# Softplus from one table function, and an LN root by Newton steps, in a fused attention and two-MLP kernel

## Chip, cores and metric

One core of a Trainium2 chip runs the kernel. The metric is device microseconds, the median of three runs. The five engines each run their own queue of instructions in order: TensorE (PE, with its weight loads as PEld), VectorE (DVE), ScalarE (ACT), GpSimd (POOL) and SyncE (SP), which issues the DMAs.

## The reference

Windowed attention, then an MLP with SoLU and layer norm, then an MLP with softplus:

```python
# q, k, v: 4 batches, 8 heads, 576 positions, 64 wide
scores = where(mask, q @ k.T / 8, -1e9)       # heads 0-3: window of 32
attn = softmax(scores); x = attn @ v          # heads 4-7: every 4th of 128
x = x reshaped to 2304 tokens x 512
h = x @ w_in1                                 # 512 x 1024
solu = h * softmax(h)
ln = (solu - mean) / sqrt(var + 1e-6) * g_ln
y = ln @ w_out1                               # 1024 x 512
h = y @ w_in2                                 # 512 x 2048
g = maximum(h, 0) + log1p(exp(-abs(h)))       # softplus
out = g @ w_out2                              # 2048 x 512
```

## The kernel before, in words

All matrices are split into a high and a low fp16 half, and each product is three matmuls (high x high, high x low, low x high). Weights are read raw, converted and scaled by VectorE and ScalarE, and kept in SBUF as fp16 halves (tile W, tile E and parts of W as working room). Attention runs in 28 pairs of blocks; `pair` takes the first ten in fp32 (`pair32`, `block32`) and the others in fp16 halves (`block`). A block has scores on TensorE, a mask and maximum on VectorE (L990), four Exp on ScalarE (`expo`, L885 and L995), halves of the result, transposed matrices by a DMA on SP's queue, values on TensorE, and a normalization.

Tokens then go through `m1` (L1075), 18 tiles of 128 tokens: 24 matmuls into a two-bank PSUM tile ps_w, a maximum (L1116), an Exp with sum (L1119), products, a Square with sum for the variance (L1127), and the root of the variance: ScalarE takes Ln and Exp of a single column (L1131 and L1132), VectorE adds one Newton step (L1134 to L1137). A normalization and a transposing DMA (lnT) follow. `y_stage` (L1160) makes y for groups of 256 tokens.

`mlp2` (L1194) does the second MLP: nine groups of 256 tokens, eight steps p each, 72 steps. A step is `hidden` (24 matmuls of 256 columns into one of two PSUM banks that y, too, uses), then the softplus into g, then `outp` (12 matmuls of 512 columns into ps_w). The softplus is seven operations: Abs (L1223, ScalarE, bank to tile a, scale invC), ReLU (L1225, ScalarE or VectorE, bank to tile r, scale KR), Exp and Ln on a (L1232 and L1233), a VectorE pass that forms KR * a + r in r (L1234), the high half of r in g as a cast (L1235, ScalarE or VectorE) and the low half r - g (L1236, VectorE). There are two buffers of a, two of r, three of g. The first two groups (`early`) take their scales by weight quarter (KR0, invD), the others one scale (KR, iD).

The order of all instructions is made by a planner, `Plan`, when the program is built. Each operation has the engines it can run on with a cost, operations it comes after, and buffers it uses. Selected steps have a due time, from the table `DUE` (L303): the pairs, m1 tiles, y, the hidden steps by weight quarter, and the weight quarters. `order` (L141) hands the due times back along the dependences and then simulates: whenever an engine is idle it takes the most urgent ready operation for which buffers are free. Where TensorE has nothing to do in the first 400 us of that simulation, eight small matmuls are put in as fillers (L1337). Every engine's queue, SP's DMAs too, follows the list that comes out; after L1332 the operations are issued in that order.

Helpers record the operations, so their lines show in the profile: L464 all ScalarE ACTIVATEs, L468 and L470 VectorE tensor_scalar, L473 scalar_tensor_tensor, L476 tensor_tensor, L497 casts, L482 matmuls, L485 transposes. The table of ScalarE's functions is loaded once, at L521.

Of the kernel before, what the change touches and what calls it, by code (L numbers as in the profile page):

```python
# [10 lines left out]
FP32 = mybir.dt.float32  # L11
# [5 lines left out]
AXX = mybir.AxisListType.X  # L17
NEG = -(2.0 ** 120)
# [42 lines left out]
class Op:  # L61
    __slots__ = ("name", "opts", "fn", "after", "uses", "due", "late", "i", "wait", "succ", "mv", "cols", "on", "t0", "t1")


class Plan:
# [11 lines left out]
    SAME = {"PE": 0.0, "ACT": 0.105, "DVE": 0.08}  # L77

# [62 lines left out]
    def order(self):  # L141
# [14 lines left out]
        moved = 0.0  # L156
        self.acts, self.fast, self.known, self.dense = [0.0], [False], [0], []
# [6 lines left out]
        while events:  # L164
# [17 lines left out]
            while again:  # L182
                again = False
                for e in self.ENGINES:
# [81 lines left out]
def kernel(  # L266
# [104 lines left out]
    KR0 = mem([128, 2, NQ], FP32, "KR0")  # L371
    KR = mem([128, 2, NQ], FP32, "KR")
# [59 lines left out]
    a_pool = pool("a", 2, [128, 2, GRP], FP32, fifo=False)  # L432
    r_pool = pool("r", 2, [128, 2, GRP], FP32, fifo=False)
# [87 lines left out]
    nc.scalar.preload_act_table_set("natural_log_exp_and_others")  # L521
# [165 lines left out]
    def w2_quarter(qd, wait_i, wait_o):  # L687
# [18 lines left out]
            lambda e: stt(KR0[:, 0, c], s2o[:, 1, c], 2.0 ** 50, t[:, 1:2], ALU.mult, ALU.mult),  # L706
            lambda e: ts(KR0[:, 1, c], KR0[:, 0, c], invC[:, c]),
        )]
        if qd == NQ - 1:
# [3 lines left out]
                lambda e: ts(KR[:, 0], s2o[:, 1], 2.0 ** 50, t[:, 2:3], ALU.mult, ALU.mult),  # L713
                lambda e: tt(KR[:, 1], KR[:, 0], invC, ALU.mult),
# [153 lines left out]
    def block32(n, o, kind, b, i, half, rows, m, nk, qt, kt, v3, qk_ops, v_ops, due):  # L868
# [16 lines left out]
        def expo(e):  # L885
# [6 lines left out]
            (act_cost(nk, ptr=1, psum=1, k=4), expo),  # L892
# [79 lines left out]
    def block(n, o, kind, b, i, half, rows, m, nk, sc, qt, kt, v2, at, qk_ops, v_ops, due, x2s):  # L972
# [22 lines left out]
        def expo(e):  # L995
# [7 lines left out]
            (act_cost(nk, ptr=1, k=4), expo),  # L1003
# [71 lines left out]
    def m1(t):  # L1075
# [31 lines left out]
        if iv is None:  # L1107
# [11 lines left out]
        ex = P.op(f"m1e{t}", act_cost(F1, ptr=2, acc=1, psum=1), lambda e: act(eb.t, ph(), ACTF.Exp, scale=x(), bias=col(1), accum_out=col(2)), after=[mx], uses=[ps, st, eb])  # L1119
# [19 lines left out]
        c1 = P.op(f"m1x{t}", TINY, lambda e: ts(col(11), col(4), col(10)), after=[cf], uses=[st])  # L1139
        c2 = P.op(f"m1y{t}", TINY, lambda e: ts(col(12), col(5), col(10)), after=[cf], uses=[st])  # L1140
# [53 lines left out]
    def mlp2(j):  # L1194
# [6 lines left out]
        for p in range(NP):  # L1201
# [5 lines left out]
            ps, ab, rb, gb = Buf(ps_y), Buf(a_pool), Buf(r_pool), Buf(g_pool)  # L1207
# [162 lines left out]
```

## Time and profile before

| | us |
|---|---|
| median of three runs | 772.73 (770.56 to 773.54) |
| span of the profiled execution, first to last instruction | 767.3 |
| TensorE busy | 722.2 |
| VectorE busy | 571.1 |
| ScalarE busy | 488.7 |

The profile is of one execution; its own time is known as its span. Busy time of TensorE counts matmuls that wait in a pipeline, so a high share is not yet full speed.

### The profile page before, as it was taken

Reading aid. Unit: us, or ns where it says so; the run is one execution under the profiler, and the core shown is the slowest. Engines: PE = TensorE matmul, PEld = TensorE weight load, DVE = VectorE, ACT = ScalarE, POOL = GpSimd, SP = SyncE. Lnnn points to the kernel's source line nnn. Section 1 sums busy time; section 2 is a strip of 40 time slices with the busy share of each in tenths; the row PEclk is TensorE's granted clock in tenths of the full one; section 3 lists DMA queues with packets and bytes.
Section 4 is the critical chain, followed back from the end, with each engine's and each line's share of the span. In section 5 each row is a group of like instructions: output and inputs, shape, how many; then the busy total and the mean of one; then the engine's idle time right before and its main releaser. Section 6 shows DMA issues by size and latency. Waiting matters only on the chain.

```text
span 767.3 us, 16330 instructions
## 1 busy us (share of the span) xinstructions
PE 722.2 (94%) x6233; PEld 516.2 (67%) x6233; DVE 571.1 (74%) x1628; ACT 488.7 (64%) x1090; POOL 3.5 (0%) x22
## 2 busy tenths in 40 slices
PE   7999789999889999989989889999999999999997
PEld 6775566767766657867646567658577576767654
DVE  2899789889999997899879999984456726433334
ACT  4576865688897777898749868964437415452513
POOL 1000000000000000000000000000000000000000
PEclk9558888999999999999999999999999999999999
DMA  9986763465977345998987787630411012000001
GB/s 212 286 270 191 195 184 90 138 129 136 177 149 133 119 122 175 208 199 157 162 161 150 125 155 138 114 59 15 109 29 28 1 24 60 1 1 1 1 28 56
DMA packets 187806, 89.94 MB, mean 117 GB/s; under 512 B 158032, under 2 KB 175440, under 8 KB 187728
## 3 DMA queue, kind: packets, MB, share of 16 engines
q1 hardware_dynamic: 187728, 88.90, 51.7%
q8 instruction: 49, 0.80, 0.4%
q14 instruction: 29, 0.24, 0.1%
HBM read 54.53 MB, written 4.72 MB: 77 GB/s over the span
## 4 chain that ended last, share of the span: by engine, by line
PE 48%; DVE 28%; ACT 9%; DMA 6%; issue 5%; SPq 1%; ACTq 0%; DVEq 0%
PE bank L482 24%; PE ps_w L482 21%; DVE W L473 5%; DVE E L473 3%; DMA pT<-p 2%; PE bank L1337 2%; ACT a L464 2%; DVE s L990 2%; ACT s L464 1%; DVE st L1116 1%; DVE r L473 1%; DMA E<-in_moe_w_out_dram 1%; DVE p L476 1%; ACT E L464 1%; DVE E L470 1%
## 5 line engine op out<-in xcount | busy, mean ns | idle before, releaser
L482 PEld LDWEIGHTS <-W 128*128 128x128 f16 x2592 | 252.4, 98 | 38.9 <-issue 3.8
L482 PE MATMUL bank<-y,W 128*128 128x256 f16 x1728 | 196.6, 274 | 3.2 <-ACT a L464 2.1
L482 PE MATMUL ps_w<-W,g 128*128 128x512 f16 x864 | 195.5, 382 | 0.5 <-DVE osb L468 0.5
L482 PEld LDWEIGHTS <-g 128*128 128x128 f16 x864 | 83.8, 99 | 94.6 <-issue 2.9
L482 PE MATMUL ps_w<-W,xr 128*128 128x512 f16 x432 | 103.3, 396 | 1.2 <-DVE osb L468 0.6
L482 PE MATMUL bank<-lnT,W 128*128 128x256 f16 x864 | 97.6, 273 | 0.0
L464 ACT ACTIVATE a<-a 128x512 f32<-128x512 f32 x144 | 90.3, 627 | 2.5
L464 ACT ACTIVATE a<-bank,invC 128x512 f32<-128x512 f32 x72 | 49.1, 681 | 64.8 <-PE bank L482 61.4
L482 PEld LDWEIGHTS <-xr 128*128 128x128 f16 x432 | 43.2, 102 | 53.1 <-issue 9.1
L473 DVE SCALAR_TENSOR_TENSOR r<-a,KR,r 128x512 f32<-128x512 f32 x72 | 53.5, 744 | 18.3 <-ACT r L464 10.5
L464 ACT ACTIVATE E<-E 128x768 f32<-128x768 f32 (+3 forms) x56 | 40.8, 729 | 27.2 <-DVE E L473 16.7
L1337 PE MATMUL bank<-eye 128*128 128x60 bf16 x1056 | 42.9, 201 | 15.6 <-DVE rs L468 4.9
L470 DVE TENSOR_SCALAR r<-bank,KR 128x512 f32<-128x512 f32 x33 | 24.7, 748 | 43.2 <-ACT a L464 38.6
L464 ACT ACTIVATE s<-s 96x128 f32<-96x128 f32 (+3 forms) x144 | 43.6, 376 | 15.7 <-DVE s L470 9.5
L1337 PEld LDWEIGHTS <-eye 128*128 128x128 bf16 x1056 | 40.3, 105 | 18.3 <-issue 18.1
L476 DVE TENSOR_TENSOR g<-r,g 128x512 f16<-128x512 f32 x72 | 49.3, 685 | 2.9
L497 DVE CAST g<-r 128x512 f16<-128x512 f32 x52 | 21.9, 422 | 31.5 <-PE ps_w L482 31.0
L464 ACT ACTIVATE r<-bank,KR 128x512 f32<-128x512 f32 x39 | 26.6, 682 | 22.8 <-DVE g L476 22.8
L990 DVE CUSTOM_DVE_ANT_0 s<-bank,band,bsc 96x128 f32<-96x128 f32 (+3 forms) x144 | 38.8, 321 | 0.7 <-DVE x L476 0.2
L482 PE MATMUL bank<-kT,qT 128*96 128x128 f16 (+7 forms) x304 | 29.9, 246 | 4.5 <-DVE s L990 3.7
L464 ACT ACTIVATE e<-ps_w,st,bsc 128x1024 f32<-128x1024 f32 x16 | 19.2, 1199 | 18.8 <-DVE st L468 11.2
L464 ACT ACTIVATE y<-bank 128x512 f16<-128x512 f32 x17 | 9.9, 587 | 31.4 <-PE bank L482 31.4
(199 smaller groups left out, 949.1 us busy)
## 6 DMA issues: line engine op xcount, KB each, us to landing
E<-in_moe_w_in_dram SPq DMA_DIRECT2D x18, 512.0 KB, 4.6
E<-in_moe_w_out_dram SPq DMA_DIRECT2D x18, 512.0 KB, 4.6
out_dram<-osb SPq DMA_DIRECT2D x18, 256.0 KB, 2.0
E<-in_q_dram SPq DMA_DIRECT2D x9, 384.0 KB, 3.2
E<-in_k_dram SPq DMA_DIRECT2D x9, 384.0 KB, 3.5
E<-in_v_dram SPq DMA_DIRECT2D x9, 384.0 KB, 3.4
W<-in_moe_w_in_dram SPq DMA_DIRECT2D x6, 512.0 KB, 5.5
W<-in_moe_w_out_dram SPq DMA_DIRECT2D x6, 512.0 KB, 5.3
```

Source lines behind the costliest of these rows:

```text
L464: pin(nc.scalar.activation(out=out, in_=in_, func=func, **kw))
L470: pin(nc.vector.tensor_scalar(out=out, in0=in0, scalar1=s1, scalar2=s2, op0=op0, op1=op1))
L473: pin(nc.vector.scalar_tensor_tensor(out=out, in0=in0, scalar=s, in1=in1, op0=op0, op1=op1, **kw))
L476: pin(nc.vector.tensor_tensor(out=out, in0=a, in1=b, op=op))
L482: pin(nc.tensor.matmul(out, l, r, start=start, stop=stop))
L497: pin(nc.vector.tensor_copy(out, in_))
L990: pin(nc.vector.tensor_tensor_reduce(out=sv()[:rows, h, :nk], in0=sb.t[:rows, h, :nk], in1=band[:rows, 48 - m:48 - m + nk], scale=sc[:rows ...
L1116: ({"DVE": (1.142, 0.14)}, lambda e: pin(nc.vector.tensor_reduce(out=col(0), in_=ph(), axis=AXX, op=ALU.max, negate=True)), [mb], [ps]),
L1337: pin(nc.tensor.matmul(banks[1][:, 452:512], eye, eye[:, 0:60], start=False, stop=False, skip_group_check=True))
```

## The change

The softplus of a step becomes three operations: Softplus on ScalarE (bank to r, scale invC), the high half scaled by KR, the low half KR * r - g on VectorE. The a buffers go, the r buffers become four. Softplus is in another table than Exp, so operations can name a table; the planner keeps track of the one loaded, charges 1.4 us for a switch (SWITCH) and treats an operation of the other table as 20 us less urgent (CLING), and a load is issued at each switch. The LN root is done by VectorE alone: a first guess by an integer shift, then three Newton steps. The due times are all new.

```diff
+TABLES = {1: "exp_and_others", 2: "softplus"}
...
+    SWITCH = 1.4
+    CLING = 20.0
...
-                    for k, (_, i) in enumerate(ready[e]):
+                    best = None
+                    for key, i in ready[e]:
                         o = self.ops[i]
+                        if best is not None and key >= best[0]:
+                            break
+                        if e == "ACT" and o.tab and o.tab != tab:
+                            key += self.CLING
+                            if best is not None and key >= best[0]:
+                                continue
...
+                    if e == "ACT" and o.tab and o.tab != tab:
+                        c += self.SWITCH
+                        tab = o.tab
...
-        "pair0": -306.26, "pair1": 456.13, "pair2": 383.87, "pair3": -398.59, "pair4": 207.99, "pair5": 302.62,
+        "pair0": 1047.13, "pair1": 1033.87, "pair2": 1015.4, "pair3": 1200, "pair4": 58.3, "pair5": 619.87,
...
-    KR0 = mem([128, 2, NQ], FP32, "KR0")
-    KR = mem([128, 2, NQ], FP32, "KR")
+    KR0 = mem([128, NQ], FP32, "KR0")
+    KR = mem([128, NQ], FP32, "KR")
...
-    a_pool = pool("a", 2, [128, 2, GRP], FP32, fifo=False)
-    r_pool = pool("r", 2, [128, 2, GRP], FP32, fifo=False)
+    r_pool = pool("r", 4, [128, 2, GRP], FP32, fifo=False)
...
-    nc.scalar.preload_act_table_set("natural_log_exp_and_others")
+    nc.scalar.preload_act_table_set("exp_and_others")
...
-            lambda e: stt(KR0[:, 0, c], s2o[:, 1, c], 2.0 ** 50, t[:, 1:2], ALU.mult, ALU.mult),
-            lambda e: ts(KR0[:, 1, c], KR0[:, 0, c], invC[:, c]),
+            lambda e: stt(KR0[:, c], s2o[:, 1, c], 2.0 ** 50, t[:, 1:2], ALU.mult, ALU.mult),
...
-        v1 = P.op(f"m1w{t}", dve_cost(0), lambda e: ts(col(7), col(6), 1.0 / F1, 1e-6, ALU.mult, ALU.add), after=[va], uses=[st])
-
-        rt = P.chain(f"m1r{t}", [
-            ({"ACT": (0.094, 0.15)}, lambda e: act(col(8), col(7), ACTF.Ln)),
-            ({"ACT": (0.094, 0.15)}, lambda e: act(col(9), col(8), ACTF.Exp, scale=-0.5)),
-        ], after=[v1], uses=[st])
+        i32 = lambda i: col(i).bitcast(INT32)
         cf = P.chain(f"m1k{t}", [(TINY, f) for f in (
+            lambda e: ts(col(7), col(6), 1.0 / F1, 1e-6, ALU.mult, ALU.add),
+            lambda e: ts(i32(9), i32(7), 1, op0=ALU.logical_shift_right),
+            lambda e: ts(i32(9), i32(9), -1.0, float(0x5F3759DF - 2 ** 31), ALU.mult, ALU.add),
             lambda e: stt(col(10), col(9), col(9), col(7), ALU.mult, ALU.mult),
-            lambda e: ts(col(10), col(10), -512.0, 1536.0, ALU.mult, ALU.add),
-            lambda e: ts(col(10), col(10), col(9)),
-        )], after=[rt], uses=[st])
+            lambda e: stt(col(9), col(10), 3.0, col(9), ALU.subtract, ALU.mult),
+            lambda e: stt(col(10), col(9), col(9), col(7), ALU.mult, ALU.mult),
+            lambda e: stt(col(9), col(10), 12.0, col(9), ALU.subtract, ALU.mult),
+            lambda e: stt(col(10), col(9), col(9), col(7), ALU.mult, ALU.mult),
+            lambda e: stt(col(10), col(10), 768.0, col(9), ALU.subtract, ALU.mult),
+        )], after=[va], uses=[st])
...
-            ab_ = P.op(f"ab{j}.{p}", act_cost(512, ptr=1, psum=1), lambda e, ps=ps, ab=ab, cq=cq: act(ab.t, ps.t, ACTF.Abs, scale=invC[:, cq]), after=[hm], uses=[ps, ab])
...
-            re = P.op(f"re{j}.{p}", {**act_cost(512, ptr=1, psum=1), **dve_cost(512, x=1.5)}, relu, after=[hm], uses=[ps, rb])
-            ee = P.op(f"ee{j}.{p}", act_cost(512), lambda e, ab=ab: act(ab.t, ab.t, ACTF.Exp, scale=-1.0), after=[ab_], uses=[ab])
-            le = P.op(f"le{j}.{p}", act_cost(512), lambda e, ab=ab: act(ab.t, ab.t, ACTF.Ln, bias=1.0), after=[ee], uses=[ab])
-            fi = P.op(f"gf{j}.{p}", dve_cost(512, x=1), lambda e, ab=ab, rb=rb, cq=cq, kr=kr: stt(rb.t, ab.t, kr[:, 0, cq], rb.t, ALU.mult, ALU.add), after=[le, re], uses=[ab, rb])
-            gh = P.op(f"gh{j}.{p}", either(512), lambda e, rb=rb, gb=gb: cast(e, gb.t[:, 0], rb.t), after=[fi], uses=[rb, gb])
-            gl = P.op(f"gl{j}.{p}", dve_cost(512), lambda e, rb=rb, gb=gb: tt(gb.t[:, 1], rb.t, gb.t[:, 0], ALU.subtract), after=[gh], uses=[rb, gb])
+            sp = P.op(
+                f"sp{j}.{p}", act_cost(512, ptr=1, psum=1),
+                lambda e, ps=ps, rb=rb, cq=cq: act(rb.t, ps.t, ACTF.Softplus, scale=invC[:, cq]), after=[hm], uses=[ps, rb], tab=2,
+            )
+            gh = P.op(
+                f"gh{j}.{p}", either(512, ptr=1),
+                lambda e, rb=rb, gb=gb, cq=cq, kr=kr: scaled(e, gb.t[:, 0], rb.t, kr[:, cq]), after=[sp], uses=[rb, gb],
+            )
+            gl = P.op(
+                f"gl{j}.{p}", dve_cost(512, x=1),
+                lambda e, rb=rb, gb=gb, cq=cq, kr=kr: stt(gb.t[:, 1], rb.t, kr[:, cq], gb.t[:, 0], ALU.mult, ALU.subtract),
+                after=[gh], uses=[rb, gb],
+            )
...
+        if o.on == "ACT" and o.tab and o.tab != tab:
+            tab = o.tab
+            pin(nc.scalar.preload_act_table_set(TABLES[tab]))
         o.fn(o.on)
```

The attention's Exp and the first MLP's Exp (L892, L1003, L1119) name table 1.

## Rows read from the trace of the kernel before

**Rows 1.** Busy time by stretch: stretch, its length, busy us of each engine (instructions), clock.

```profile
0.00:100.00 100.00, 85.07 (x743) 65.72 (x744) 75.47 (x200) 65.26 (x190) 3.52 (x22) 0.73 0.81 227
100.00:200.00 100.00, 92.75 (x941) 70.87 (x940) 92.33 (x289) 71.33 (x178) 0.00 (x0) 0.93 0.58 138
200.00:505.00 305.00, 286.90 (x2716) 203.15 (x2715) 277.80 (x896) 243.92 (x542) 0.00 (x0) 0.99 0.76 150
505.00:767.30 262.30, 257.51 (x1836) 176.49 (x1836) 125.47 (x248) 108.17 (x182) 0.00 (x0) 1.00 0.12 29
```

The engines stand in the order PE, PEld, DVE, ACT, POOL; after the clock come the DMA share and GB/s.

**Rows 2.** Chain of waits, shares by line, from 200 to 505 us and from 505 us.

```profile
by line: PE ps_w L482 12.1%; PE bank L482 12.1%; issue 8.5%; DMA pT<-p 5.4%; ACT a L464 4.2%; DVE s L990 3.7%; DVE E L473 3.4%; ACT s L464 3.2%; DVE W L473 2.4%; DVE r L473 2.3%; DVE p L476 2.2%; PE bank L1337 2.1%; DVE st L1116 1.9%; DMA E
...
by line: PE bank L482 51.8%; PE ps_w L482 46.4%; DVE osb L468 0.3%; ACT osb L464 0.3%; issue 0.0%
```

**Rows 3.** Busy time by stretch of the filler matmuls' line L1337 alone: PE, PEld.

```profile
100.00:200.00 100.00, 10.90 (x281) 10.13 (x281) 0.93 0.58 138
200.00:505.00 305.00, 13.49 (x432) 12.76 (x431) 0.99 0.76 150
```

**Rows 4.** Groups of instructions the change removes or alters: busy us, mean ns, idle before.

```profile
L464 ACT ACTIVATE a<-a 128x512 f32<-128x512 f32 x144 | 90.3, 627 | 2.5
L473 DVE SCALAR_TENSOR_TENSOR r<-a,KR,r 128x512 f32<-128x512 f32 x72 | 53.5, 744 | 18.3 <-ACT r L464 10.5 <-ACT a L464 7.7
L476 DVE TENSOR_TENSOR g<-r,g 128x512 f16<-128x512 f32 x72 | 49.3, 685 | 2.9
L464 ACT ACTIVATE a<-bank,invC 128x512 f32<-128x512 f32 x72 | 49.1, 681 | 64.8 <-PE bank L482 61.4 <-DVE r L473 1.7 <-DVE r L470 1.6
L464 ACT ACTIVATE r<-bank,KR 128x512 f32<-128x512 f32 x39 | 26.6, 682 | 22.8 <-DVE g L476 22.8
L470 DVE TENSOR_SCALAR r<-bank,KR 128x512 f32<-128x512 f32 x33 | 24.7, 748 | 43.2 <-ACT a L464 38.6 <-PE bank L482 3.4
L464 ACT ACTIVATE st<-st 128x1 f32<-128x1 f32 x36 | 7.0, 195 | 1.1 <-DVE st L470 0.7
```

**Rows 5.** Groups that resemble what is added, and the casts of before.

```profile
L497 DVE CAST g<-r 128x512 f16<-128x512 f32 x52 | 21.9, 422 | 31.5 <-PE ps_w L482 31.0
L464 ACT ACTIVATE g<-r 128x512 f16<-128x512 f32 x20 | 12.4, 619 | 2.6 <-DVE r L473 2.4
L473 DVE SCALAR_TENSOR_TENSOR W<-E,s2o,W 128x512 f16<-128x512 f32 x16 | 11.2, 743 | 0.0
L464 ACT ACTIVATE W<-E,s2o 128x512 f16<-128x512 f32 x11 | 7.2, 708 | 0.0
L473 DVE SCALAR_TENSOR_TENSOR st<-st 128x1 f32<-128x1 f32 x36 | 6.4, 178 | 1.6 <-ACT st L464 1.4
L468 DVE TENSOR_SCALAR W<-E,s2o 128x512 f16<-128x512 f32 x5 | 2.2, 480 | 0.0
```

**Rows 6.** Busy time by stretch of tile KR's instructions, then of tile a's: DVE, ACT.

```profile
200.00:505.00 305.00, 36.55 (x55) 11.57 (x17) 0.99 0.76 150
...
200.00:505.00 305.00, 23.66 (x33) 62.75 (x99) 0.99 0.76 150
```

**Rows 7.** Tile hl from 200 to 505 us: ns min/median/max, first and last start.

```profile
L464 ACT ACTIVATE hl<-e,st x9: 1226/1237/1254, 206.5 to 483.1; 128x1024 f16<-128x1024 f32 x9
```

**Rows 8.** Timeline of ScalarE, its first instruction: start us, duration us.

```profile
0.80 1.28 ACT L521 ACT_TABLE_LOAD   x1 [0.80 <-PEq L1354]
```

**Rows 9.** Timeline of ScalarE: Abs and attention's Exp in turn, first and last.

```profile
205.96 0.69 ACT L464 ACTIVATE a<-bank,invC 128x512 f32<-128x512 f32 x1 [0.43 <-PE bank L482]
...
208.86 1.23 ACT L464 ACTIVATE s<-s 80x112 f32<-80x112 f32 x4
...
499.60 0.67 ACT L464 ACTIVATE a<-bank,invC 128x512 f32<-128x512 f32 x1
```

**Rows 10.** Chain of waits in order of time: start us, us, the two longest waits on weight loads.

```profile
68.91 3.59 DMA E<-in_moe_w_out_dram
...
139.34 4.88 DMA E<-in_moe_w_out_dram
```

More of the change, by code (lines that the diff above doesn't have):

```diff
@@ L61 @@
 class Op:
-    __slots__ = ("name", "opts", "fn", "after", "uses", "due", "late", "i", "wait", "succ", "mv", "cols", "on", "t0", "t1")
+    __slots__ = ("name", "opts", "fn", "after", "uses", "due", "late", "i", "wait", "succ", "mv", "cols", "tab", "on", "t0", "t1")
 class Plan:
@@ L81, in __init__, with op @@
         self.due = due
-    def op(self, name, opts, fn, after=(), uses=(), due=None, mv=0, cols=0.0):
+    def op(self, name, opts, fn, after=(), uses=(), due=None, mv=0, cols=0.0, tab=0):
         o = Op()
-        o.name, o.opts, o.fn, o.due, o.mv, o.cols = name, opts, fn, due, mv, cols
+        o.name, o.opts, o.fn, o.due, o.mv, o.cols, o.tab = name, opts, fn, due, mv, cols, tab
         o.after = [a for a in dict.fromkeys(after) if a is not None]
@@ L102, in chain @@
             w = [*(after if o is None else [o]), *(more[0] if more else [])]
-            o = self.op(f"{name}{'abcdefghijklmnop'[i]}", opts, fn, w, [*uses, *(more[1] if len(more) > 1 else [])])
+            o = self.op(f"{name}{'abcdefghijklmnop'[i]}", opts, fn, w, [*uses, *(more[1] if len(more) > 1 else [])], tab=more[2] if len(more) > 2 else 0)
         return o
@@ L156, in order @@
         moved = 0.0
+        tab = 1
         self.acts, self.fast, self.known, self.dense = [0.0], [False], [0], []
@@ L196, in order @@
                                 continue
-                        got = []
+                        got, slots = [], []
                         for b in o.uses:
@@ L205, in order @@
                                 got.append(b)
+                                slots.append(s)
                         else:
-                            break
+                            best = (key, o, list(zip(got, slots)))
                         for b in reversed(got):
@@ L210, in order @@
                             b.pool.next -= 1
-                    else:
+                        if best is not None and e != "ACT":
+                            break
+                    if best is None:
                         continue
+                    _, o, got = best
+                    i, c = o.i, o.opts[e][0]
+                    for b, s in got:
+                        b.slot, s[4][0] = s, True
+                        b.pool.next += 1
                     for f in o.opts:
@@ L712, in w2_quarter @@
                 lambda e: recip(t[:, 2:3], iD),
[L713 to L714 removed]
+                lambda e: ts(KR, s2o[:, 1], 2.0 ** 50, t[:, 2:3], ALU.mult, ALU.mult),
             )]
@@ L891, in block32 @@
             (TINY, lambda e: ts(nm()[:rows], mx()[:rows], -scale)),
-            (act_cost(nk, ptr=1, psum=1, k=4), expo),
+            (act_cost(nk, ptr=1, psum=1, k=4), expo, [], [], 1),
         ], after=[qk_mm], uses=[sb, s2])
@@ L1002, in block @@
             (TINY, lambda e: ts(nm()[:rows], mx()[:rows], -1.0, shift, ALU.mult, ALU.add)),
-            (act_cost(nk, ptr=1, k=4), expo),
+            (act_cost(nk, ptr=1, k=4), expo, [], [], 1),
         ], after=[mk], uses=[s2])
@@ L1118, in m1 @@
         ], after=[iv_ok[b0], iv_ok[b1]], uses=[st])
-        ex = P.op(f"m1e{t}", act_cost(F1, ptr=2, acc=1, psum=1), lambda e: act(eb.t, ph(), ACTF.Exp, scale=x(), bias=col(1), accum_out=col(2)), after=[mx], uses=[ps, st, eb])
+        ex = P.op(f"m1e{t}", act_cost(F1, ptr=2, acc=1, psum=1), lambda e: act(eb.t, ph(), ACTF.Exp, scale=x(), bias=col(1), accum_out=col(2)), after=[mx], uses=[ps, st, eb], tab=1)
         rc = P.chain(f"m1c{t}", [
@@ L1206, in mlp2 @@
                 po = Buf(ps_w)
-            ps, ab, rb, gb = Buf(ps_y), Buf(a_pool), Buf(r_pool), Buf(g_pool)
+            ps, rb, gb = Buf(ps_y), Buf(r_pool), Buf(g_pool)
             cq = slice(qd, qd + 1)
@@ L1222, in mlp2 @@
             hm = P.op(f"h{j}.{p}", pe_cost(2.62), hidden, cols=6.1, after=[*y_ops[j], *need], uses=[ps, yb], due=(f"h{j}.{qd}", d))
-            ab_ = P.op(f"ab{j}.{p}", act_cost(512, ptr=1, psum=1), lambda e, ps=ps, ab=ab, cq=cq: act(ab.t, ps.t, ACTF.Abs, scale=invC[:, cq]), after=[hm], uses=[ps, ab])
-            def relu(e, ps=ps, rb=rb, cq=cq, kr=kr):
-                if e == "ACT":
-                    act(rb.t, ps.t, ACTF.Relu, scale=kr[:, 1, cq])
-                else:
-                    ts(rb.t, ps.t, kr[:, 1, cq], 0.0, ALU.mult, ALU.max)
-            re = P.op(f"re{j}.{p}", {**act_cost(512, ptr=1, psum=1), **dve_cost(512, x=1.5)}, relu, after=[hm], uses=[ps, rb])
-            ee = P.op(f"ee{j}.{p}", act_cost(512), lambda e, ab=ab: act(ab.t, ab.t, ACTF.Exp, scale=-1.0), after=[ab_], uses=[ab])
-            le = P.op(f"le{j}.{p}", act_cost(512), lambda e, ab=ab: act(ab.t, ab.t, ACTF.Ln, bias=1.0), after=[ee], uses=[ab])
-            fi = P.op(f"gf{j}.{p}", dve_cost(512, x=1), lambda e, ab=ab, rb=rb, cq=cq, kr=kr: stt(rb.t, ab.t, kr[:, 0, cq], rb.t, ALU.mult, ALU.add), after=[le, re], uses=[ab, rb])
-            gh = P.op(f"gh{j}.{p}", either(512), lambda e, rb=rb, gb=gb: cast(e, gb.t[:, 0], rb.t), after=[fi], uses=[rb, gb])
-            gl = P.op(f"gl{j}.{p}", dve_cost(512), lambda e, rb=rb, gb=gb: tt(gb.t[:, 1], rb.t, gb.t[:, 0], ALU.subtract), after=[gh], uses=[rb, gb])
+            sp = P.op(
[11 more added lines that the diff above has]
+            )
             def outp(e, p=p, po=po, gb=gb, first=first, last=last):
@@ L1332 @@
     order = P.order()
+    tab = 1
     mm(banks[1][:, 452:512], eye, eye[:, 0:60], True, True)
```

4 lines of the change are left out of this document (2 added, 2 removed), and 30 rows, old and new, of the table DUE.

## The prediction

> **What bounds the kernel now.** I read the busy time by stretch first. The run has three parts [rows 1]. Up to 200 us it starts up: TensorE's granted clock is 0.73 and then 0.93 (a mixture of its levels 1.2 and 2.4 GHz), while weights and attention inputs come in. From 200 to 505 us attention, first MLP and second MLP run mixed: VectorE is busy 277.8 of 305 us (91.1%), ScalarE 243.9 (80%), TensorE 286.9. From 505 us on TensorE is busy 257.5 of 262.3 us at clock 1.00, with VectorE and ScalarE under half busy.
>
> The chain of waits says the same. In the last part 98% of it is TensorE's matmuls of the two MLPs; in the mixed part these matmuls hold only 24%, and the rest is scattered over VectorE, ScalarE and small DMAs of attention [rows 2]. So a faster softplus is worth nothing after 505 us, where its engines wait for TensorE anyway. It is worth what it shortens the mixed part by, as long as TensorE still does the same work there. TensorE can give up what it loses in that part: 305 - 286.9 = 18.1 us idle and 13.5 us of filler matmuls [rows 1, 3], 31.6 us together. That is a ceiling for the mixed part.
>
> **What the change removes.** The second MLP has 72 steps. Each loses an Exp and a Ln on ScalarE (627 ns each), a ReLU (682 ns on ScalarE 39 times, 748 ns on VectorE 33 times) and the combining pass on VectorE (744 ns); the Abs becomes Softplus on the same operands, which I leave at Abs's 681 ns: ReLU with the same kinds of operands takes 682, Exp and Ln are alike, so the function seems not to matter [rows 4]. Bounds are the nearest rows, 627 and 748 ns, or 33 x 0.07 = 2 us of ScalarE either way. In the mixed part 33 steps run; the tiles show it exactly: 36.6 us of VectorE and 11.6 us of ScalarE write r with KR, and of the 62.8 us on tile a, 33 x 0.681 = 22.5 us stays, so 40.3 us goes [rows 6].
>
> **What it adds.** The low half becomes the form with a scalar pointer, 743 instead of 685 ns; the high half takes a scale, 480 instead of 422 ns on VectorE or 708 instead of 619 ns on ScalarE [rows 4, 5]. For 33 steps that is 1.9 us, and at most 1.9 us of VectorE or 2.9 us of ScalarE. The LN root: two ScalarE operations of 195 ns go [rows 4], and nine one-column VectorE operations stand for four, so 5 x 178 ns = 0.89 us per tile [rows 5]. Nine of the 18 tiles fall in the mixed part [rows 7]: 8.0 us of VectorE, 3.5 us of ScalarE saved. The chain of an LN tile is longer by 0.89 - 0.39 = 0.5 us. Five one-column operations on weight scales go too, under 1 us in all.
>
> VectorE in the mixed part: 36.6 - 1.9 - 1.9 - 8.0 = 24.8 us less. ScalarE: 40.3 + 11.6 + 3.5 - 2.9 = 52.5 us less, before table loads.
>
> **Table loads.** The trace has one load, 1.28 us, at the start; Exp and Ln then share a table [rows 8]. Now each passage between an Exp (attention, first MLP) and a Softplus takes a load. Taking Abs as the place of Softplus, I counted in ScalarE's order of before 57 passages, 45 of them between 200 and 505 us, from the first to the last shown [rows 9]. At 1.28 us that is 57.6 us, so ScalarE is 5 us worse off there than before (249.0 against 243.9), though still 18% idle. The new planner holds an operation of the other table back by 20 us of urgency, which makes passages fewer; but it takes one when nothing else is ready. I keep 45. Below, a passage costs the load alone; above, the load and the emptying of ScalarE, which is at most its longest common instruction, 1.24 us [rows 7], so 2.52 us. I take the low end, the only row of a load itself; that load is ScalarE's first instruction, so it has nothing to empty and can't settle it. Behind a load wait ScalarE's later instructions in order: an attention Exp and with it VectorE's halves and the transposing DMA on SP's queue, or a Softplus and with it the TensorE step that wants its PSUM bank. Before 200 us four passages and after 505 us eight fall in idle time; what covers them there is that ScalarE is 68% and 41% busy; uncovered they would be 15 us.
>
> What the Trainium skill, "ScalarE: Activation LUTs", section "What ACT_TABLE_LOAD costs", states speaks against the change: a switch is 1.28 us of load and 1.38 us of drain, 2.66 us. The load agrees with the trace; no run here shows the drain. By it the 45 passages would be 120 us and the time an estimated 809 us. Its section "Rules for kernel authors" says to keep Exp and Ln in their common table and not to switch, which is the kernel before.
>
> **The order.** All due times are new, so every pair, MLP tile, y and hidden step and weight quarter may move in the queues of TensorE, ScalarE, VectorE and SP, with its four loads per weight half. Data still fixes most of it: no step of the second MLP runs before its weight quarter and LN tile. What it does to the start I cannot work out. The largest waits on a weight load in the chain are 3.6 and 4.9 us [rows 10]; one more or one fewer of each gives a bound of 8.5 us both ways, and I take zero. The r buffers go from two to four in the room of the dropped a buffers, and a PSUM bank is free after one reader, not two; I cost this at nothing because it only removes waits.
>
> **The sum.** Above: VectorE keeps its 91.1% filling, and the mixed part shrinks by 24.8 / 0.911 = 27 us, inside the ceiling of 31.6. Below: only what stood on the chain goes. ScalarE's work on tile a is 4.2% of 305 us there, 12.8 us, of which 40.3 / 62.8 or 8.2 us goes; the combining pass is 2.3%, 7.0 us [rows 2]; less 0.5 us for each of nine LN tiles, 11 us. I take the middle, 19 us, as neither end is nearer: the upper needs TensorE to lose almost nothing any more. Start and end stay. The profiled execution has a span of 767.3 us, so 748.3 us after; the median of the runs, 772.7, is 5.4 us above that span, and I carry this along: **753.7, say 754 us**, by itself 745 to 762.
>
> **Rivals.**
> *Larger gain.* A second-MLP step now asks VectorE for half as much, so the new order can start it earlier and put it where TensorE ran fillers or stood idle from 100 to 200 us as well: 7.2 + 10.9 us [rows 1, 3]. With two thirds of that and the full 27 us: 772.7 - 39 = 733 us. Against it: VectorE is 92% busy there with weights.
> *The load lands on the chain.* Attention's Exp is 3.2% of the chain, 9.8 us or eight groups of 1.23 us, and some eight Softplus stand there in place of the 12.8 us on tile a [rows 2, 9]. A load before each is 16 x 1.28 = 20 us, which eats the gain: 773 us. For it: the chain is made of latencies. Against: the planner knows of the switch and holds back.
> *Slower: ScalarE fills up.* It has 243.9 - 52.5 = 191.4 us left in the mixed part and may be as full as VectorE is now, 277.8 us. So 86 us of loads fit, and the point of decision is 45 passages of 1.9 us. At 2.52 us they are 113 us, ScalarE needs 304.8 / 0.911 = 335 us, and the kernel takes 30 us longer, 802 us; with some passages saved, some 790.
> *Not the change it says.* If the Softplus table did not hold Copy, Identity and Square too, each Softplus would need a load on both sides: 33 x 2 x 1.28 = 84.5 us, which just fits ScalarE but lies on the chain as above: about 773 us. The trace shows one table that serves everything [rows 8], not this one. The Trainium skill, on the same page, "Table sets: the hidden batching unit", says that every set holds the cheap functions; no run here shows it.
>
> **How the numbers follow.** A difference under 0.5% (3.9 us) can't be told from none, so same is 769 to 777 us. Forecast 0.52, larger gain 0.17, load on the chain 0.12, two loads each 0.03, ScalarE full 0.16. Faster: 0.52 + 0.17 = 0.69; same: 0.12 + 0.03 = 0.15; slower: 0.16. The range 733 to 777 leaves out the slower case and little more. The forecast alone is 745 to 762, and 737 to 771 with the start's 8.5 us.
>
> **What would show it.** Right: tile a and the combining pass gone, some 30 to 57 table loads of 1.28 us, VectorE's busy time about 571 - 54 = 517 us in all (78.2 us on r [rows 4], less 72 x 0.116 and 18 x 0.89), the stretch in which TensorE is full beginning near 485 us and as long as before, fewer idle and filler microseconds ahead of it. Wrong: ScalarE over 91% in the mixed part, or gaps beside the loads as long as themselves (slower); the chain of waits led through table loads (same); Softplus much over 681 ns; or a start that is longer by more than one weight load.

## The result, and the profile after

The changed kernel takes 749.6 us (median of four, 746.9 to 751.3) beside 772.5 us of the kernel before: ratio 0.9717 (95% interval 0.9686 to 0.9748), 2.8% faster. The forecast was 754 us, in a range of 733 to 777. The profiled execution took 749.8 us with a span of 748.0, so 1.8 us lie around the span.

Busy time by stretch of the kernel after (columns as in [rows 1]: stretch, length, PE, PEld, DVE, ACT, POOL, clock, DMA share, GB/s):

```profile
0.00:100.00 100.00, 83.75 (x855) 66.61 (x856) 79.16 (x216) 68.84 (x186) 3.52 (x22) 0.78 0.78 221
100.00:200.00 100.00, 90.11 (x854) 70.40 (x851) 88.19 (x268) 63.55 (x158) 0.00 (x0) 0.90 0.50 140
200.00:505.00 305.00, 295.80 (x2460) 209.15 (x2458) 252.22 (x820) 208.88 (x387) 0.00 (x0) 1.00 0.67 141
505.00:748.00 243.00, 237.41 (x1738) 160.72 (x1735) 113.00 (x329) 104.78 (x157) 0.00 (x0) 1.00 0.23 44
```

The fillers alone, stretches as in [rows 3] and the first 100 us; behind them that first stretch of the kernel before, which [rows 3] leaves out:

```profile
0.00:100.00 100.00, 23.16 (x472) 22.02 (x472) 0.78 0.78 221
100.00:200.00 100.00, 8.72 (x214) 7.96 (x210) 0.90 0.50 140
200.00:505.00 305.00, 1.42 (x40) 1.35 (x40) 1.00 0.67 141
```

```profile
0.00:100.00 100.00, 18.48 (x344) 17.43 (x344) 0.73 0.81 227
```

The gain can be read here. After 200 us TensorE used to lose 18.1 + 4.8 us idle and 13.5 us of fillers [rows 1, 3], 36.4 us in all. Now it loses 9.2 + 5.6 us and 1.4 us, 16.2 us. The difference, 20.2 us, covers the 19.3 us that the span is shorter; the matmuls after 200 us that are no fillers are busy 0.9 us longer. The start gave nothing: TensorE is idle 26.1 us of the first 200 (22.2 before) and runs fillers for 31.9 (29.4 before).

But the shape isn't the one forecast. The forecast was that the mixed part gets shorter, with as long a stretch behind it as before in which TensorE alone is full. Attention does not end sooner. The groups of ScalarE's Exp on tile s, of the kernel before and of the kernel after (ns min/median/max, first and last start):

```profile
L464 ACT ACTIVATE s<-s x144: 344/375/404, 181.2 to 510.3; 96x128 f32<-96x128 f32 x56, 80x112 f32<-80x112 f32 x48, 80x80 f32<-80x80 f32 x32, 96x96 f32<-96x96 f32 x8
```

```profile
L485 ACT ACTIVATE s<-s x144: 345/374/402, 232.7 to 605.5; 96x128 f32<-96x128 f32 x56, 80x112 f32<-80x112 f32 x48, 80x80 f32<-80x80 f32 x32, 96x96 f32<-96x96 f32 x8
```

The last attention Exp moved from 510 to 606 us. The new order spreads attention thinner: between 200 and 505 us stand 38 Softplus (33 Abs before) and 108 of these Exp (121 before). TensorE is busy 97% of that time (94% before), VectorE 83% (91% before). The chain of waits from 200 to 505 us and from 505 us, shares by line as in [rows 2], is now:

```profile
by line: PE bank L503 31.1%; PE ps_w L503 22.8%; issue 4.3%; DMA pT<-p 3.8%; DMA E<-in_v_dram 2.9%; DVE E L494 2.4%; DMA qT<-qk 2.0%; DVE s L1009 2.0%; ACT L1361 1.8%; DMA E<-in_q_dram 1.7%; DVE g L494 1.4%; SPq L512 1.4%; ACT s L485 1.4%; 
...
by line: PE ps_w L503 45.7%; PE bank L503 42.6%; ACT L1361 2.1%; DVE s L1009 1.8%; ACT s L485 1.4%; ACT r L485 0.9%; issue 0.7%; DVE osb L489 0.6%; ACT g L485 0.6%; ACT osb L485 0.5%; DVE st L1135 0.5%; DVE g L494 0.3%; DVE v L494 0.3%; DVE
```

TensorE's matmuls (L503) hold 54% of the chain from 200 to 505 us, where they held 24% [rows 2]: TensorE now sets most of the time there too. Table loads (L1361) hold 1.8 and 2.1%.

The costliest groups that answer to [rows 4, 5] (busy us, mean ns, idle before):

```profile
L1361 ACT ACT_TABLE_LOAD x61 | 78.3, 1283 | 1.1
L494 DVE SCALAR_TENSOR_TENSOR g<-r,KR,g 128x512 f16<-128x512 f32 x72 | 53.8, 747 | 52.6 <-ACT g L485 51.4
L485 ACT ACTIVATE r<-bank,invC 128x512 f32<-128x512 f32 x72 | 49.0, 685 | 64.8 <-PE bank L503 62.8 <-DVE g L494 1.6
...
L485 ACT ACTIVATE g<-r,KR 128x512 f16<-128x512 f32 x40 | 28.7, 721 | 1.3 <-PE ps_w L503 0.2
...
L489 DVE TENSOR_SCALAR g<-r,KR 128x512 f16<-128x512 f32 x32 | 15.4, 481 | 9.8 <-PE ps_w L503 7.0 <-ACT r L485 2.6
```

Softplus takes 685 ns (681 forecast), the low half 747 (743), the high half 721 on ScalarE (708) and 481 on VectorE (480). There are 61 table loads of 1283 ns behind the first one (57 counted in the old order), 5 of them before 200 us, 36 from 200 to 505 us (45 forecast) and 20 later. The timeline of ScalarE around some of them (start us, us):

```profile
230.66 0.69 ACT L485 ACTIVATE r<-bank,invC 128x512 f32<-128x512 f32 x1 [0.82 <-PE bank L503]
231.37 1.28 ACT L1361 ACT_TABLE_LOAD   x1
232.66 1.28 ACT L485 ACTIVATE s<-s 96x128 f32<-96x128 f32 x4
233.96 1.28 ACT L1361 ACT_TABLE_LOAD   x1
235.25 0.69 ACT L485 ACTIVATE r<-bank,invC 128x512 f32<-128x512 f32 x1
235.96 1.28 ACT L1361 ACT_TABLE_LOAD   x1
...
249.68 0.69 ACT L485 ACTIVATE r<-bank,invC 128x512 f32<-128x512 f32 x1
250.26 0.83 ACT L485 ACTIVATE E<-E 128x768 f32<-128x768 f32 x1
```

Every one of the 61 loads begins about 0.02 us after the end of the instruction ahead of it, and 52 are followed as closely. Without a load between them, neighbours overlap: the Square (E<-E) at 250.26 begins 0.11 us before the end of the Softplus at 249.68. So a switch takes some 1.4 us of ScalarE, the load, two short gaps and the lost overlap, which is what SWITCH charges.

### The profile page after: what moved, and what is told of

Read it like the earlier page. It is cut to its first block, busy times and chain, and to the rows that moved or that the text cites. A ratio compares the mean times of both kernels' runs of the same rounds, so it can differ in the third digit from the quotient of the medians.

```text
span 748.0 us, 15440 instructions
## 1 busy us (share of the span) xinstructions
PE 707.1 (95%) x5897; PEld 506.9 (68%) x5897; DVE 532.6 (71%) x1631; ACT 446.0 (60%) x885; POOL 3.5 (0%) x22
## 4 chain that ended last, share of the span: by engine, by line
PE 56%; DVE 21%; DMA 7%; ACT 7%; issue 3%; SPq 1%; ACTq 0%; DVEq 0%
PE bank L503 29%; PE ps_w L503 26%; DVE W L494 5%; DVE E L494 2%; DMA pT<-p 2%; ACT L1361 1%; DVE s L1009 1%; DMA E<-in_moe_w_in_dram 1%; DMA E<-in_v_dram 1%; PE bank L1357 1%; ACT s L485 1%; DMA qT<-qk 1%; DVE g L494 1%; DVE st L494 1%; DVE st L1135 1%
## 5 line engine op out<-in xcount | busy, mean ns | idle before, releaser
L503 PEld LDWEIGHTS <-W 128*128 128x128 f16 x2592 | 252.5, 98 | 39.1 <-issue 3.4
L503 PE MATMUL bank<-y,W 128*128 128x256 f16 x1728 | 197.2, 273 | 0.9 <-ACT r L485 0.9
L503 PE MATMUL ps_w<-W,g 128*128 128x512 f16 x864 | 195.0, 379 | 1.4 <-DVE osb L494 1.0
L503 PEld LDWEIGHTS <-g 128*128 128x128 f16 x864 | 83.1, 98 | 92.4 <-issue 1.7
L503 PE MATMUL ps_w<-W,xr 128*128 128x512 f16 x432 | 100.1, 387 | 0.0
L503 PE MATMUL bank<-lnT,W 128*128 128x256 f16 x864 | 98.2, 274 | 1.9 <-ACT r L485 1.6
L494 DVE SCALAR_TENSOR_TENSOR g<-r,KR,g 128x512 f16<-128x512 f32 x72 | 53.8, 747 | 52.6 <-ACT g L485 51.4
L485 ACT ACTIVATE r<-bank,invC 128x512 f32<-128x512 f32 x72 | 49.0, 685 | 64.8 <-PE bank L503 62.8
L1361 ACT ACT_TABLE_LOAD x61 | 78.3, 1283 | 1.1
L503 PEld LDWEIGHTS <-xr 128*128 128x128 f16 x432 | 42.8, 100 | 49.1 <-issue 3.9
L485 ACT ACTIVATE y<-bank 128x512 f16<-128x512 f32 x18 | 10.6, 591 | 60.7 <-PE bank L503 60.7
L1357 PE MATMUL bank<-eye 128*128 128x60 bf16 x720 | 33.3, 209 | 13.0 <-DVE xr L497 3.6
L494 DVE SCALAR_TENSOR_TENSOR y<-bank,y 128x512 f16<-128x512 f32 x18 | 12.4, 686 | 43.6 <-ACT y L485 43.6
L1357 PEld LDWEIGHTS <-eye 128*128 128x128 bf16 x720 | 31.3, 111 | 15.6 <-issue 15.1
L503 PE MATMUL bank<-kT,qT 128*96 128x128 f16 (+7 forms) x320 | 30.6, 242 | 1.8 <-DVE s L1009 1.8
L1135 DVE TENSOR_REDUCE st<-ps_w 128x1 f32<-128x1024 f32 x18 | 21.9, 1218 | 11.8 <-PE ps_w L503 11.8
L485 ACT ACTIVATE g<-r,KR 128x512 f16<-128x512 f32 x40 | 28.7, 721 | 1.3 <-PE ps_w L503 0.2
L494 DVE SCALAR_TENSOR_TENSOR E<-E 128x512 int32<-128x512 int32 x42 | 27.3, 686 | 0.1
```

What stands on the lines that cost most here:

```text
L485: pin(nc.scalar.activation(out=out, in_=in_, func=func, **kw))
L494: pin(nc.vector.scalar_tensor_tensor(out=out, in0=in0, scalar=s, in1=in1, op0=op0, op1=op1, **kw))
L503: pin(nc.tensor.matmul(out, l, r, start=start, stop=stop))
L1135: ({"DVE": (1.142, 0.14)}, lambda e: pin(nc.vector.tensor_reduce(out=col(0), in_=ph(), axis=AXX, op=ALU.max, negate=True)), [mb], [ps]),
L1357: pin(nc.tensor.matmul(banks[1][:, 452:512], eye, eye[:, 0:60], start=False, stop=False, skip_group_check=True))
L1361: pin(nc.scalar.preload_act_table_set(TABLES[tab]))
```

## The experiments

Each kernel was timed beside the kernel before on the same chip, so ratios are compared; 0.001 of ratio is 0.8 us. "Against" is the difference of ratios times 772.5 us, to the kernel whose order it has.

| run | ratio (95% interval) | against |
|---|---|---|
| kernel after | 0.9717 (0.9686 to 0.9748) | |
| no loads | 0.9643 (0.9603 to 0.9682) | -5.7 us, after |
| two loads | 1.0193 (1.0144 to 1.0242) | +36.8, after |
| two to Softplus | 0.9936 (0.9911 to 0.9962) | +16.9, after |
| two to Exp | 0.9871 (0.9830 to 0.9911) | +11.9, after |
| low half twice | 0.9997 (0.9965 to 1.0028) | +21.6, after |
| Softplus thrice | 1.0366 (1.0318 to 1.0413) | +50.1, after |
| old load, new order | 1.0702 (1.0648 to 1.0755) | +76.1, after |
| two Newton steps | 0.9675 (0.9639 to 0.9710) | -3.2, after |
| no Exp and Ln | 0.9960 (0.9937 to 0.9984) | -3.1, before |
| no combining | 0.9942 (0.9918 to 0.9966) | -4.5, before |
| neither | 0.9883 (0.9832 to 0.9934) | -9.0, before |
| Newton, old order | 1.0165 (1.0122 to 1.0208) | +12.7, before |

### What the table loads cost

No loads, and ReLU for Softplus:

```diff
-                lambda e, ps=ps, rb=rb, cq=cq: act(rb.t, ps.t, ACTF.Softplus, scale=invC[:, cq]), after=[hm], uses=[ps, rb], tab=2,
+                lambda e, ps=ps, rb=rb, cq=cq: act(rb.t, ps.t, ACTF.Relu, scale=invC[:, cq]), after=[hm], uses=[ps, rb], tab=2,
...
-            pin(nc.scalar.preload_act_table_set(TABLES[tab]))
```

> The kernel after in its own order, with no table load issued after the first, and ReLU (which Exp's table holds) in the place of Softplus; so the softplus itself is left out. Theory 'hidden': ScalarE has room and the loads cost their 78 us in idle time: within 3 us of the kernel after (747 to 750 us, ratio 0.967 to 0.971). Rival 'on the chain': the loads hold 1.9% of the chain from 200 to 485 us and 2.0% of it afterwards, 5.4 + 5.3 = 10.7 us, and that comes back: about 739 us, ratio 0.957. Rival 'load and emptying': if a switch cost 2.5 us and not 1.28, more than 11 us come back.

746.0 us by its median, 3.5 us under the kernel after; 5.7 us by ratios, some 2 to 10 us with both intervals. That lies between "hidden" and "on the chain", and is little of 78 us: in this order the loads are nearly hidden. What an order made without loads would give was not tried; by the runs further down it can be more than taking them out of this one gave. Without them ScalarE is busy 162.0 us between 200 and 505 us:

```profile
200.00:505.00 305.00, 299.69 (x2480) 210.72 (x2479) 252.24 (x823) 161.96 (x350) 0.00 (x0) 1.00 0.68 141
```

Two loads at each switch:

```diff
             tab = o.tab
+            pin(nc.scalar.preload_act_table_set(TABLES[3 - tab]))
             pin(nc.scalar.preload_act_table_set(TABLES[tab]))
```

> The kernel after in its own order, with two table loads at each of the 61 switches, first the other table, then the wanted one: 78 us more of ScalarE. 'Hidden': within 4 us of the kernel after (up to 754 us). 'On the chain': 10 to 20 us longer (760 to 770 us, ratio 0.984 to 0.997), since what waits behind one load waits behind two.

788.3 us: 36.8 us longer, more than either theory gave. The first 78 us of loads cost 5.7, the second 78 cost six times that. ScalarE isn't full: it is busy 247.4 of 305 us from 200 to 505 us:

```profile
200.00:505.00 305.00, 281.48 (x2285) 196.36 (x2285) 243.04 (x794) 247.35 (x407) 0.00 (x0) 0.98 0.66 137
```

What changed is who waits. TensorE's longest waits from 200 us on, of the kernel after and of this one (who waited for whom: us, times, longest):

```profile
PE bank L503 <- DVE xf L497: 3.0, 3, 1.4
PE bank L503 <- ACT r L485: 2.5, 3, 1.6
PE bank L503 <- DVE s L1009: 1.8, 3, 0.7
```

```profile
PE bank L503 <- ACT r L485: 11.8, 8, 2.9
PE bank L503 <- DVE s L1009: 8.1, 4, 3.4
```

TensorE waits for Softplus to read a bank, 2.5 us in the kernel after and 11.8 now, and for attention's mask on VectorE, 1.8 and 8.1. These two rows are 15.6 of the 37 us; the rest is spread over waits that were not followed up. To tell these apart the second load was put ahead of one kind of switch only, `if tab == 2` or `if tab == 1` before the added line.

> The kernel after in its own order with two loads only at the switches to Softplus (31 of 61), 40 us more of ScalarE. Doubling all gave 38.8 us. If ScalarE's time is what counts, whoever waits: about half, 18 to 22 us longer than the kernel after. If the wait is TensorE's for its PSUM banks behind Softplus: nearly all of it, 28 us and more. If it is attention's Exp that is late: under 12 us.

> The same with two loads only at the switches to Exp (30 of 61), 38 us more of ScalarE. ScalarE's time: 18 to 22 us longer than the kernel after. Banks behind Softplus: under 12 us. Attention's Exp: 28 us and more.

16.9 and 11.9 us: nobody's wait alone, and each less than the 18 to 22 us expected. By microsecond added, 0.42 and 0.31; both together cost 36.8, more than the sum of 28.8. So ScalarE's time counts in either place, and more the more there is.

### The old order with less work

In the order of before, operations of the softplus are left out; the planner still counts them, so nothing else moves:

```diff
-            ee = P.op(f"ee{j}.{p}", act_cost(512), lambda e, ab=ab: act(ab.t, ab.t, ACTF.Exp, scale=-1.0), after=[ab_], uses=[ab])
-            le = P.op(f"le{j}.{p}", act_cost(512), lambda e, ab=ab: act(ab.t, ab.t, ACTF.Ln, bias=1.0), after=[ee], uses=[ab])
-            fi = P.op(f"gf{j}.{p}", dve_cost(512, x=1), lambda e, ab=ab, rb=rb, cq=cq, kr=kr: stt(rb.t, ab.t, kr[:, 0, cq], rb.t, ALU.mult, ALU.add), after=[le, re], uses=[ab, rb])
+            ee = P.op(f"ee{j}.{p}", act_cost(512), lambda e: None, after=[ab_], uses=[ab])
+            le = P.op(f"le{j}.{p}", act_cost(512), lambda e: None, after=[ee], uses=[ab])
+            fi = P.op(f"gf{j}.{p}", dve_cost(512, x=1), lambda e: None, after=[le, re], uses=[ab, rb])
```

> The order of the kernel before, with Exp, Ln and the combining pass of the softplus left out of all 72 steps (so the softplus is incomplete): 90.3 us of ScalarE and 53.5 us of VectorE less, and no table switch. Theory 'relief': the mixed part shrinks by the 24.6 us of VectorE that its 33 steps lose, as far as TensorE has lost time to give (31.6 us): 745 to 752 us. Theory 'order': engines in a fixed order only lose what stood on the chain, 8.2 us of Exp and Ln and 7.0 us of combining: 757 to 765 us. If both are wrong: 768 to 773.

765.0 us: 9.0 us by ratios (7.7 by medians), the smallest gain that "order" allowed (757 to 765 us) and far from the "relief" figure. Its waits beside those of the kernel before (columns as above), the kernel before first:

```profile
ACT a L464 <- PE bank L482: 61.4, 31, 13.8
...
DVE g L497 <- PE ps_w L482: 31.0, 12, 5.0
```

```profile
ACT a L464 <- PE bank L482: 86.9, 35, 13.8
DVE g L497 <- PE ps_w L482: 54.5, 22, 6.7
```

The engines that were relieved spend the time waiting for TensorE, 25.5 and 23.5 us more in these two rows: TensorE's queue still follows the old list. Between 200 and 505 us TensorE is busy 288.6 us, against 286.9 [rows 1]:

```profile
200.00:505.00 305.00, 288.64 (x2745) 204.85 (x2745) 263.41 (x879) 212.20 (x486) 0.00 (x0) 1.00 0.74 150
```

The two parts alone:

> The order of the kernel before, with only Exp and Ln of the softplus left out (so the softplus is incomplete): 90.3 us of ScalarE less, 41 us of it between 200 and 505 us. Leaving out these and the combining pass gave 7.7 us. Theory 'VectorE' (the forecast: ScalarE's relief counts for nothing by itself): 0 to 2 us less than the kernel before. Rival 'latency': the two are a link of each step's chain, and most of the 7.7 us comes back here.

> The order of the kernel before, with only the combining pass left out (so the softplus is incomplete): 53.5 us of VectorE less, 24.6 us of it between 200 and 505 us. 'VectorE': 6 to 8 us less than the kernel before, nearly all that both together gave. 'Latency': 2 to 4 us, by the shorter chain of a step alone.

3.1 us for 90.3 us of ScalarE, 4.5 us for 53.5 us of VectorE. By their intervals these are 1.2 to 4.9 and 2.6 to 6.3 us; they add up to about the 9.0. ScalarE's relief is worth something by itself, so "VectorE" with nothing for ScalarE is unlikely; which of the two gave more is not settled.

### The new order with more work

```diff
-                lambda e, ps=ps, rb=rb, cq=cq: act(rb.t, ps.t, ACTF.Softplus, scale=invC[:, cq]), after=[hm], uses=[ps, rb], tab=2,
+                lambda e, ps=ps, rb=rb, cq=cq, n=3 + (p % 3 == 0): [act(rb.t, ps.t, ACTF.Relu, scale=invC[:, cq]) for _ in range(n)], after=[hm], uses=[ps, rb], tab=2,
...
-                lambda e, rb=rb, gb=gb, cq=cq, kr=kr: stt(gb.t[:, 1], rb.t, kr[:, cq], gb.t[:, 0], ALU.mult, ALU.subtract),
+                lambda e, rb=rb, gb=gb, cq=cq, kr=kr, n=2 + (p % 3 == 0): [stt(gb.t[:, 1], rb.t, kr[:, cq], gb.t[:, 0], ALU.mult, ALU.subtract) for _ in range(n)],
...
-            pin(nc.scalar.preload_act_table_set(TABLES[tab]))
```

> The order of the kernel after, with about the work per step of the kernel before: no table loads, ReLU in the place of Softplus, issued three times (four times in every third step), and the low half two times (three times in every third step), 1.6 us of ScalarE and 1.0 us of VectorE more in each of the 72 steps; softplus is left out. Theory 'relief' (the saved work of VectorE gave the gain): back to 765 to 775 us. Theory 'order' (the new due times gave it, and would have with the old work): 750 to 756 us. Half and half: about 760.

828.0 us, 55 us slower than the kernel before. Both theories were far too low. But the run has more to do than the kernel before, as its page shows:

```profile
PE 726.4 (88%) x5897; PEld 508.1 (62%) x5897; DVE 606.2 (74%) x1730; ACT 480.5 (58%) x995; POOL 3.5 (0%) x22
```

VectorE is busy 606.2 us in all, 35 us more than in the kernel before (571.1), ScalarE 480.5 (488.7). The repeated passes also hold the PSUM bank, which Exp and Ln did not. So the 55 us overstate what the new order costs with the old work. One engine at a time, by `for _ in range(2)` on the low half and `range(3)` on Softplus:

> The kernel after, in its own order, with the low half computed twice in each step: 53.8 us more of VectorE. Theory 'the order is cut to its work': VectorE's 747 ns per step that the planner did not count push back everything behind them, 20 to 45 us longer than the kernel after (770 to 795 us). 'VectorE' as an amount of work: 35 steps between 200 and 485 us, 26 us, over 85% filling, 25 to 30 us longer at most. 'Not the work': under 8 us.

> The kernel after, in its own order, with Softplus issued three times on the same data in each step: 99 us more of ScalarE, about the Exp, Ln and part of the ReLU that the change took away. If ScalarE's relief was not needed: up to 10 us longer (760 us). If the new order can only exist with ScalarE's time free for loads: 35 to 60 us longer (785 to 810 us), as with the doubled loads (78 us more of ScalarE gave 39).

53.8 us more of VectorE cost 21.6 us, 99 us more of ScalarE 50.1 us. Taking out the like amounts in the old order had given 4.5 and 3.1 us. By these slopes, 0.40 and 0.51 us per us, what separates the two kernels, 38.5 us of VectorE (571.1 - 532.6) and 42.7 us of ScalarE (488.7 - 446.0), would cost an estimated 37 us if it were put back, more than the 22 us gained. So the new order is no gift of its own: it works with the freed engines. With the low half twice, VectorE is nearly as busy from 200 to 505 us as in the kernel before (277.8 us [rows 1]):

```profile
200.00:505.00 305.00, 287.79 (x2379) 201.96 (x2377) 274.65 (x855) 205.27 (x382) 0.00 (x0) 0.99 0.66 140
```

The whole time is that of the kernel before, too. That shows that VectorE's work counts in the new order, not that it alone sets the time: ScalarE is busy 38.7 us less there than in the kernel before, and more work on it counts as well.

### The LN root

The order of before, with the guess and the three steps, eight VectorE operations, in the slots of the three that followed ScalarE's root, and nothing in ScalarE's two slots (the second and third slot take two operations each, left out below):

```diff
-            ({"ACT": (0.094, 0.15)}, lambda e: act(col(8), col(7), ACTF.Ln)),
-            ({"ACT": (0.094, 0.15)}, lambda e: act(col(9), col(8), ACTF.Exp, scale=-0.5)),
+            ({"ACT": (0.094, 0.15)}, lambda e: None),
+            ({"ACT": (0.094, 0.15)}, lambda e: None),
...
-            lambda e: stt(col(10), col(9), col(9), col(7), ALU.mult, ALU.mult),
-            lambda e: ts(col(10), col(10), -512.0, 1536.0, ALU.mult, ALU.add),
-            lambda e: ts(col(10), col(10), col(9)),
+            lambda e: [
+                ts(i32(9), i32(7), 1, op0=ALU.logical_shift_right),
+                ts(i32(9), i32(9), -1.0, float(0x5F3759DF - 2 ** 31), ALU.mult, ALU.add),
+                stt(col(10), col(9), col(9), col(7), ALU.mult, ALU.mult),
+                stt(col(9), col(10), 3.0, col(9), ALU.subtract, ALU.mult),
+            ],
...
```

> The order of the kernel before with only the LN root changed to Newton steps on VectorE, the rest as before: per tile five one-column VectorE operations more, two ScalarE ones less. The forecast took 0.5 us more on each LN tile's chain, nine tiles in the mixed part, and 8.0 us of VectorE there: 1 to 8 us longer than the kernel before. If tiles wait for something else anyway: within 1 us of it. By the runs that left work out, VectorE's 53.5 us gave 4.5 us back, so 16 us should cost some 1 to 3.

12.7 us longer: a miss, over the 1 to 8 us expected and four times the 1 to 3 that the other runs had suggested. From the end of a tile's Square to its normalization it takes 0.84 us longer on average than in the kernel before (0.3 to 1.3 in the 18 tiles), not 0.5; in the nine tiles of the mixed part that makes 8.2 us. Whether this path or the 16 us more of VectorE sets the price was not separated. In the kernel after the same operations look different in VectorE's timeline; here some of one tile's, with the rest and other work left out between:

```profile
220.90 0.14 DVE L489 TENSOR_SCALAR st<-st 128x1 int32<-128x1 int32 x1
...
221.09 0.15 DVE L491 TENSOR_SCALAR st<-st 128x1 int32<-128x1 int32 x1
...
222.00 0.21 DVE L494 SCALAR_TENSOR_TENSOR st<-st 128x1 f32<-128x1 f32 x1
...
225.17 0.15 DVE L494 SCALAR_TENSOR_TENSOR st<-st 128x1 f32<-128x1 f32 x1
...
228.98 0.23 DVE L494 SCALAR_TENSOR_TENSOR st<-st 128x1 f32<-128x1 f32 x1
```

The planner puts the nine steps singly between other operations, here over 9 us. This tile is the slowest of the 18: from Square to normalization it takes 11.8 us, where the median is 3.2 (5.3 in the kernel before). What the steps cost there was tried from the other side, with one step less in the order of after:

```diff
-            lambda e: stt(col(9), col(10), 12.0, col(9), ALU.subtract, ALU.mult),
-            lambda e: stt(col(10), col(9), col(9), col(7), ALU.mult, ALU.mult),
-            lambda e: stt(col(10), col(10), 768.0, col(9), ALU.subtract, ALU.mult),
+            lambda e: stt(col(10), col(10), 12.0, col(9), ALU.subtract, ALU.mult),
+            lambda e: None,
+            lambda e: None,
...
```

> The kernel after in its own order, with two Newton steps for the LN root and not three (the root keeps a relative error of some millionths): two one-column VectorE operations less in each of the 18 LN tiles, 36 x 0.18 = 6.5 us. If the root's operations count as much here as they did in the order of before, where 16 us of them cost 12.4 us: about 5 us less than the kernel after (745 us, ratio 0.965). If work taken out of an order that is cut to it pays little, as 53.5 us of the combining pass gave 4.5 us: under 1 us (749 us, ratio 0.970 to 0.972).

745.4 us, the lowest of the kernels that compute everything: 3.2 us under the kernel after by ratios, for 6.5 us taken out. The intervals overlap, so that it beats the kernel after is likely and not settled, and the result lies between the two expectations. It is clearly faster than the kernel before.

## Why the prediction was right or wrong

**The time and the ceiling: right; the shape: not.** The gain came where it was looked for, from what TensorE loses after the start, and stayed under the ceiling of 31.6 us for the mixed part (18.1 + 13.5 us there went to 9.2 + 1.4, 21 us less). The span, forecast at 748.3 us, is 748.0. The 5.4 us carried along were 1.8 us around the span and 3.6 us by which the one profiled execution before lay under the median, so carrying them put the forecast too high. But the mixed part did not shrink, and VectorE did not keep its 91% filling: it is at 83%, and attention runs on to 606 us. VectorE's 252.2 us from 200 to 505 us equal the forecast 277.8 - 24.8 = 253.0 by chance: they are another mixture of work, over 305 us.

**The sizes: right, but for VectorE's total.** Softplus, the halves and a load came within 2%, the number of loads within 7% in all, though 36 fell into the mixed part and not 45. VectorE in all is at 532.6 us, not 517: the planner gave it work that can run on either engine (among it 27 casts of tile p instead of 16, 15 of hl instead of 9, 17 normalizations instead of 11), while ScalarE took 40 high halves instead of 20.

**The step that failed is "Above" and "Below" of the sum**, that relief shortens the mixed part, at least by what stood on the chain, 8.2 us of Exp and Ln and 7.0 us of combining, and at most by VectorE's 24.8 us at unchanged filling. Relief alone gave 3.1 and 4.5 us, and 9.0 together (5.1 to 13.0 by the interval), of the 15.2 us that stood on the chain. An entry in the chain of waits is not time that comes back: when it shrinks, another wait takes its place, in the run without both parts the two waits for TensorE's matmuls. What shortened the kernel in its place is an order that keeps TensorE fed after 200 us, 36.4 us lost before and 16.2 after, and that needs the freed engines. The root was mis-sized the other way: 0.5 us for each of nine tiles, 4.5 us, where the tiles' own paths grew by 8.2 us and the kernel by 12.7 when it was tried alone in the old order.

How the gain divides between relief and due times is not shown. Adding up what was measured apart, -9.0 + 12.7 and 5.7 for loads, the parts without a new order would make the kernel some 9 us slower, and the new due times would be worth some 31 us. That is an estimate with weak footing: separate runs did not add up above (28.8 against 36.8), the 5.7 us come from an order made with the loads in it, ReLU and the two more r buffers are left out, and the new parts with the old due times weren't tried in one kernel. That the median came within 5 us is luck in part: the forecast took order at zero and relief at 19.

**ScalarE's relief entered the sum only in its low end; it is also what pays the loads.** The forecast set 52.5 us of relief against 57.6 us of loads and had ScalarE at 249.0 us in the mixed part. With 36 loads (46 us) there it is at 208.9 us from 200 to 505 us. That room is needed: with 99 us put back the kernel is 1.0366 of the kernel before.

**The rivals.** *ScalarE fills up* gave 790 to 802 us for switches of 2.52 us; with a second load at each switch the kernel took 788. The time is near, but not for the rival's reason: ScalarE was busy 81% of the mixed part and not full. Its condition was absent, too: a switch costs about 1.4 us. The Trainium skill, "ScalarE: Activation LUTs", section "What ACT_TABLE_LOAD costs", gives a switch 1.28 us of load and 1.38 us of drain. The load agrees with the trace (1283 ns); a drain of that length shows nowhere in it, where loads begin 0.02 us behind the instruction ahead and most are followed as closely. *The load lands on the chain* was to eat 20 us; the loads do stand on the chain (1.8% of 305 us and 2.1% of 243 us, 10.6 us), but 5.7 us is what taking them away returned. *Two loads for each Softplus* did not occur: 61 loads serve 72 Softplus, and the Square above follows a Softplus without one. The Trainium skill, "ScalarE: Activation LUTs", section "Table sets: the hidden batching unit", says that every set holds the cheap functions, copy and identity among those it names; it does not name Square there. *Larger gain* did not come: the start's idle time and fillers stayed.

## What to carry to other kernels

In this kernel, whose order is cut to its work, freeing an engine paid little until the order was made anew, and added work that the order did not count was paid for at 31 to 79% of its length in the six runs that add one kind of it. So cost a change to such a kernel as relief and reordering together, and don't judge a part by switching it on in the old order. Read the gain from what the bounding engine loses (idle time and fillers), not from the share of the chain. A second function table was cheap where ScalarE had room for the loads in the order itself: taking out 78 us of planned loads gave 6 us, putting in 78 us of unplanned ones cost 37.

## What was not expected of the hardware

A table load follows the instruction ahead of it within 0.03 us, 61 times of 61, and takes little of ScalarE beyond its 1283 ns: the gaps and the lost overlap of neighbours, some 0.1 us. The steep price of unplanned work was a surprise too: 16 us of one-column VectorE operations cost 12.7 us, more than the 4.5 us that 53.5 us of full passes gave back when they were taken out of the same order.
